# Squared-ReLU feed-forward after retention: the second product with its weights stationary and 192 tokens moving

## The chip, the cores and the metric

The kernel runs on one core of a Trainium2 chip. The metric is the device time of one execution in microseconds (us). The profiled execution is a single one, taken by the hardware profiler; its engines are called TensorE (PE; its weight loads PEld), VectorE (DVE), ScalarE (ACT), GpSimd (POOL) and SyncE (SP), whose queue issues nearly all DMAs here.

## The reference

```python
# q, k, v: (8, 8, 576, 64) float32; w_in: (512, 2048), w_out: (2048, 512)
scores = scale * np.matmul(q, k.transpose(0, 1, 3, 2))
Dmat = np.where(rel >= 0, gamma[:, None, None] ** rel[None, :, :], 0.0)
attn_out = np.matmul(scores * Dmat[None, :, :, :], v)
x = attn_out.transpose(0, 2, 1, 3).reshape(B * S, H * D)     # (4608, 512)
h = np.maximum(x @ w_in, 0.0)
return (h * h @ w_out).astype(np.float32)                    # (4608, 512)
```

All of it is float32. The weights come in as 64-bit floats, which the kernel reads as 64-bit integers and converts itself.

## The kernel before

The 4,608 tokens are nine blocks of 512. The work has two stages.

The first stage (up to about 548 us) computes retention in chunks of 128 tokens and, block by block, g = relu(x w_in)^2. It also loads w_out in sixteen pieces (`fetch_w`, L204, source pattern `piece_src`, L184), converts them on VectorE and forms seven combinations of its quarters, twice over: the result, `w2_dram`, holds for each of seven outer products the seven inner right operands. A piece is asked for when the piece three before it is finished (L275). g is written to DRAM as `g_dram`: of each half-block of 256 tokens' operand combinations five are kept (`G_KEPT`: A11, S1, A12, S3, A22). The order in this stage is written out by hand: `ffn` (L801) hands out a number of steps for each chunk, and a step carries the DMA issues that are due.

The second stage (L922 to L1128) computes g w_out by a scheme that replaces eight block products by seven (`PRODUCTS`, L27), on two levels. The outer level splits a block's tokens in two halves of 256, w_out's 2,048 rows in two and its 512 columns in two. The left operands are A11, S2, S1, A12, S3, S4, A22 of g. Five are read by `fetch_g` (L940) into one of six buffers `A(k)`; S2 and S4 are made on VectorE as differences of two others (`made`, L947, four quarters each). The inner level does the same again: `inner_sums` (L962) forms S1 to S4 of the quarters of A(k) on VectorE, and `inner(k, i)` (L1003) does inner product i. Each is four matmuls over chunks of 128 rows: 128 tokens of g stationary, 128 columns of w_out moving (L1017), so a result has tokens on the partitions. `k` counts outer products: nine blocks times seven, 63, and the blocks are taken in the order 1 to 8, then 0.

The inner results stay in three accumulators in PSUM per k and are combined with `p1`, `u2` and `p15`: product 0 and 3 leave through ScalarE (L1025, L1031), the others by an addition on VectorE (L1027 to L1037) into `r`. `outer` (L1068) adds `r` into the output tile on VectorE (L1079) and sends out a finished half-block of 256 tokens in one DMA on SyncE's queue (L1083). The very last product goes by `last_inner` (L1039), which adds quarter by quarter and sends each off.

The loop at L1104 sets the order. In iteration k TensorE gets inner products 0, then 4 of k - 1, 1 of k, 5 of k - 1, 2 of k, 6 of k - 1, 3 of k. Between them VectorE's queue gets the inner sums of k + 1, differences for k + 2, and steps of `sums_0` (L981), which forms S1 and S3 of block 0 from stored quarters (L996). At the end of an iteration the operand of k + 4 is asked for. The weights of the outer product j lie in `w_out[j]`, read by `fetch_w2` (L616).

At the border of the stages the last block's steps carry the first reads of g, the four inner sums of product 0 and four differences for product 1 (L1087 to L1099).

Of the kernel before, what the change touches and what calls it, by code (L numbers as in the profile page):

```python
# [17 lines left out]
TOK = 512  # L18
# [18 lines left out]
CLOSES = {3, 5, 6}  # L37


@with_exitstack  # L40
def kernel(
# [142 lines left out]
    def piece_src(j):  # L184
        wi, m, e = pieces[j]
        f = (m + e * N_M) * 128
        if wi == 0:
            return moe_w_in.rearrange("(c p) f -> p c f", p=128)[:, :, f:f + 128]
        return moe_w_out[f:f + 128, :].rearrange("p (c f) -> p c f", c=N_DM)
# [14 lines left out]
    def fetch_w(j):  # L204
        if j < len(pieces) and wide:
            nc.sync.dma_start(raw_of(j).bitcast(I64).rearrange("p (c f) -> p c f", c=N_DM), piece_src(j))
# [4 lines left out]
    def round_parts(j):  # L211
        words = raw_of(j).bitcast(U32).rearrange("p (n two) -> p n two", two=2)
        lo, hi = words[:, :, 0], words[:, :, 1]
        exp = exp_of(j).bitcast(U32)
        t = piece_dst(j)
        bits = t.bitcast(U32)

        def one():
            nc.vector.tensor_scalar(exp, hi, 20, 0x7FF, op0=ALU.logical_shift_right, op1=ALU.bitwise_and)

        def two():

            nc.vector.tensor_scalar(bits, as_dst(j, hi), 0xFFFFF, 0x100000, op0=ALU.bitwise_and, op1=ALU.bitwise_or)

        def beside():

            nc.scalar.activation(exp, exp, AF.Relu, bias=exp_bias[:, 0:1], scale=2.0 ** 23)

        def three():
            nc.vector.scalar_tensor_tensor(t, as_dst(j, lo), 2.0 ** -32, bits, op0=ALU.mult, op1=ALU.add)  # L230

        def four():
            nc.vector.scalar_tensor_tensor(t, t, 2.0 ** -20, as_dst(j, exp_of(j)), op0=ALU.mult, op1=ALU.mult)

        def five():
            nc.vector.scalar_tensor_tensor(bits, as_dst(j, hi), 0x80000000, bits, op0=ALU.bitwise_and, op1=ALU.bitwise_or)

        if not wide:
            to = t if pieces[j][0] == 0 else t.rearrange("p o s f -> p (o s) f")
            return [lambda: nc.sync.dma_start(to, piece_src(j))] + [lambda: None] * 5  # L240
        return [one, two, beside, three, four, five]
# [374 lines left out]
    def fetch_w2(j):  # L616
        nc.sync.dma_start(w_out[j].rearrange("p m s f -> p m (s f)"), w2_dram[WO_SLOT[PRODUCTS[j][1]], :, :, :])
# [310 lines left out]
    def part(at):  # L928
        return room[:, at:at + N_M * HT]

    A_room = [late.tile([128, N_M * HT], F32, name=f"a{j}") for j in range(4)] + [part(2048), part(4096)]
    s_room = [part(11776), part(0), part(13824)]
    o_room = [part(at).rearrange("p (h j d) -> p h j d", h=2, j=2) for at in (7168, 9216)]
    N_K = N_BLK * NP
    BLOCKS = list(range(1, N_BLK)) + [0]

    def A(k):
        return A_room[k % len(A_room)].rearrange("p (m t) -> p m t", m=N_M)

    def fetch_g(k):  # L940

        j = k % NP
        if k < N_K and j not in (2, 5):
            k += j == 1
            nc.sync.dma_start(A(k), g_dram[BLOCKS[k // NP], G_KEPT.index(PRODUCTS[k % NP][0]), :, :, :])

    def made(k):  # L947

        if k >= N_K or k % NP not in (1, 5):
            return []  # L950
        x, y = (k + 1, k - 1) if k % NP == 1 else (k - 2, k - 4)
        at = [slice(2 * e, 2 * e + 2) for e in range(4)]
        return [lambda at=at: nc.vector.tensor_tensor(A(k)[:, at, :], A(x)[:, at, :], A(y)[:, at, :], op=ALU.subtract) for at in at]

    def lefts(k):

        x = A(k)
        t = s_room[k % 3].rearrange("p (s m t) -> p s m t", s=4, m=N_MQ)
        return dict({f"S{e + 1}": t[:, e, :, :] for e in range(4)},
                    A11=x[:, 0:N_MQ, 0:128], A12=x[:, N_MQ:, 0:128], A21=x[:, 0:N_MQ, 128:], A22=x[:, N_MQ:, 128:])  # L960

    def inner_sums(k):  # L962

        if k >= N_K:
            return [None] * 4
        x = lefts(k)
        return [
            lambda: nc.vector.tensor_tensor(x["S1"], x["A21"], x["A22"], op=ALU.add),
            lambda: nc.vector.tensor_tensor(x["S2"], x["S1"], x["A11"], op=ALU.subtract),
            lambda: nc.vector.tensor_tensor(x["S3"], x["A11"], x["A21"], op=ALU.subtract),  # L970
            lambda: nc.vector.tensor_tensor(x["S4"], x["A12"], x["S2"], op=ALU.subtract),
        ]
# [3 lines left out]
    def bank(name):  # L976
        n_bank[0] += 1
        pool, tag = (ps_f, "f") if n_bank[0] % 8 < 3 else (ps_g, "g")
        return pool.tile([128, 512], F32, tag=tag, name=name)[:, 0:128]

    def sums_0():  # L981

        for m in range(N_M):
# [9 lines left out]
            for _ in range(6):  # L993
                yield None
# [3 lines left out]
            for _ in range(3):  # L998
                yield None

    state = {}

    def inner(k, i):  # L1003

        n, j = divmod(k, NP)
        o = o_room[n % 2]
        if i == 0:
            small = late3.tile([128, 3, 128], F32, tag="small", name="small")
            r = o[:, 0, :, 0:HT] if j == 0 else late2.tile([128, 2, HT], F32, tag="r", name="r")
            state[k] = dict(r=r, lefts=lefts(k), p1=small[:, 0, :], u2=small[:, 1, :], p15=small[:, 2, :])  # L1010
# [5 lines left out]
        for m in range(N_MQ):  # L1016
            nc.tensor.matmul(p, lhsT=s["lefts"][left][:, m, :], rhs=w_out[j][:, m, WO_SLOT[right], :],  # L1017
# [3 lines left out]
        if k == N_K - 1:  # L1021

# [7 lines left out]
        elif i == 3:  # L1030
            nc.scalar.copy(r[:, 0, 0:128], p)  # L1031
        elif i == 4:
            nc.vector.tensor_tensor(r[:, 1, 128:], p, s["p15"], op=ALU.add)
        elif i == 5:
            nc.vector.tensor_tensor(r[:, 0, 128:], p, s["u2"], op=ALU.add)
        else:
            nc.vector.tensor_tensor(r[:, 1, 0:128], p, s["p1"], op=ALU.add)  # L1037

    def last_inner(s, i, p):  # L1039
        n = N_BLK - 1  # L1040
        o = o_room[n % 2]
        c21 = o[:, 1, :, 0:HT]
        add = lambda to, x, y: nc.vector.tensor_tensor(to, x, y, op=ALU.add)
        at = {3: (0, 0), 4: (1, 1), 5: (0, 1), 6: (1, 0)}
        place = lambda e: c21[:, at[e][0], 128 * at[e][1]:128 * at[e][1] + 128]
        if i == 0:
            nc.scalar.copy(s["p1"], p)
        elif i == 1:
            add(s["u2"], p, s["p1"])
            add(s["u2"], s["u2"], place(5))  # L1050
        elif i == 2:
            add(s["p15"], p, s["p1"])
            add(s["p15"], s["p15"], place(4))
            add(s["p1"], s["p1"], place(6))
        else:
            add(place(i), p, {3: place(3), 4: s["p15"], 5: s["u2"], 6: s["p1"]}[i])
        def leave(rows, cols):
            row = BLOCKS[n] * TOK + HT + rows * 128
            nc.sync.dma_start(out[row:row + 128, cols], o[:, 1, rows, cols])

        if i == 3:
            leave(0, slice(HT, TOK))
            leave(1, slice(HT, TOK))
        if i >= 3:
            rows, c = at[i]
            leave(rows, slice(128 * c, 128 * c + 128))

    def outer(k):  # L1068

        if k == N_K - 1:  # L1070
            return
        n, j = divmod(k, NP)
        r = state.pop(k)["r"]
        o = o_room[n % 2]
        c11, c12 = o[:, 0, :, 0:HT], o[:, 0, :, HT:]
        c21, c22 = o[:, 1, :, 0:HT], o[:, 1, :, HT:]
        for to, with_ in {1: [(c21, c11)], 2: [(c12, c21)], 3: [(c11, c11)], 4: [(c22, c12), (c21, c21)],
                          5: [(c12, c12)], 6: [(c21, c21)]}.get(j, []):
            nc.vector.tensor_tensor(to, r, with_, op=ALU.add)  # L1079
        if j >= 5:  # L1080
            half = j - 5
            row = BLOCKS[n] * TOK + half * HT
            nc.sync.dma_start(out[row:row + HT, :].rearrange("(a p) d -> p a d", p=128), o[:, half, :, :])  # L1083
# [3 lines left out]
    while steps:  # L1087
        n, f, *args = steps[0]
        if n == N_BLK - 1:
            if n_last in (0, 5, 10, 15):  # L1090
                fetch_g(n_last // 5)
            if n_last in (2, 9, 16, 23):
                fetch_w2(2 + n_last // 7)
            if n_last == N_MP * NP - 5:
                for f in inner_sums(0):
                    f()
            if n_last >= N_MP * NP - 4:
                made(1)[n_last - N_MP * NP]()
# [5 lines left out]
    for k in range(N_K + 1):  # L1104
        sums_g = [None] * (k % NP == NP - 1) + made(k + 2)
        assert k + 4 < N_K - NP or next(steps_0, None) is None
        sums_next = inner_sums(k + 1)
        if k < N_K:
            inner(k, 0)
        for e in range(3):  # L1110
            if k > 0:
                inner(k - 1, 4 + e)
            if e == 2 and k > 0:
                outer(k - 1)
            if k < N_K:
                inner(k, 1 + e)
            if sums_next[e]:
                sums_next[e]()
            if sums_g:
                f = sums_g.pop(0)  # L1120
            else:
                f = next(steps_0, None)
            f and f()
        if sums_next[3]:
            sums_next[3]()
        for f in sums_g:
            f()
        fetch_g(k + 4)  # L1128
# [46 lines left out]
```

## Time and profile before

| | |
|---|---|
| time, median of 3 runs | 947.91 us (946.22 to 948.93) |
| profiled execution, its own time | 948.14 us |
| its span, first to last instruction | 946.4 us |
| mean granted TensorE clock | 0.998 |
| TensorE busy | 936.4 us (99%) |
| weight loads busy | 843.4 us (89%) |
| VectorE busy | 764.1 us (81%) |
| ScalarE busy | 353.9 us (37%) |
| GpSimd busy | 83.1 us (9%) |
| moved by DMA | 181.42 MB |

The profile's page lists groups of instructions by line of code, with count, busy time and mean duration of one. The views by time say what an engine did in a stretch. A busy matmul is not a matmul at its peak: its end is modelled and overlaps the next one, so what counts is the distance from one start to the next. The same holds in part for VectorE. The chain of work that ended last is followed back from the last instruction, at each step to what released it; 95% of it is TensorE.

### The profile page before, as it was taken

The numbers are of one execution on the slowest core, as the hardware profiler recorded it, in microseconds if no ns is written. First come the engines' busy times: TensorE is split into PE (matmuls) and PEld (weight loads), VectorE is DVE, ScalarE is ACT, GpSimd is POOL, SyncE is SP. The second block draws the span as 40 slices with busy tenths as digits, with TensorE's granted clock in tenths as the row PEclk, the third lists the DMA queues.
The fourth block names the chain that finished last, engine by engine and source line by source line (L and its number), as shares of the span: only waits on it lengthen the run. The fifth ranks groups of instructions, "written<-read, shape, count | busy, mean of one in ns | idle before, by whom it ended". The sixth has DMA issues, their size and how long they took to land.

```text
span 946.4 us, 23257 instructions
## 1 busy us (share of the span) xinstructions
PE 936.4 (99%) x9724; PEld 843.4 (89%) x9724; DVE 764.1 (81%) x1419; ACT 353.9 (37%) x831; POOL 83.1 (9%) x82
## 2 busy tenths in 40 slices
PE   8999999999999999999999999999999999999998
PEld 7554878888888888888888899999999999999998
DVE  5978699979797988888846688888878788787876
ACT  3557767676676686676621110000000000000000
POOL 3223011111111111220000000000000000000000
PEclk9999999999999999999999999999999999999999
DMA  9997475686468565863569983544555453525241
GB/s 223 230 281 194 143 196 144 193 289 190 148 201 273 176 190 163 276 190 117 186 224 361 347 294 124 189 161 142 192 179 185 158 206 107 201 101 178 110 160 46
DMA packets 173673, 181.42 MB, mean 192 GB/s; under 512 B 119168, under 2 KB 134400, under 8 KB 166912
## 3 DMA queue, kind: packets, MB, share of 16 engines
q1 hardware_dynamic: 171472, 179.41, 59.8%
q8 instruction: 76, 1.25, 0.5%
q10 hardware_dynamic: 2096, 0.52, 0.3%
q14 instruction: 29, 0.24, 0.1%
HBM read 109.39 MB, written 70.52 MB: 190 GB/s over the span
## 4 chain that ended last, share of the span: by engine, by line
PE 95%; DVE 3%; DMA 1%; ACT 0%; issue 0%; SPq 0%; DVEq 0%
PE o_b L1017 18%; PE h_b L706 17%; PE o_c L1017 12%; PE o_a L1017 12%; PE h_a L706 12%; PE h_c L706 11%; PE h_ps L668 6%; PE x_ps L565 3%; PE sc_ps L471 2%; PE x_ps L600 1%; PE u_ps L559 1%; DMA q_ld<-in_q_dram 1%; PE sc_ps L500 0%; PE t_ps L436 0%; PE x_ps L526 0%
## 5 line engine op out<-in xcount | busy, mean ns | idle before, releaser
L706 PE MATMUL h_b<-room,w 128*128 128x256 f32 x768 | 181.6, 379 | 1.3 <-DVE room L725 1.3
L422 ACT COPY qk<-flip 32x256 f32<-32x256 f32 x432 | 173.8, 402 | 6.7
L706 PEld LDWEIGHTS h_b<-room,w 128*128 128x128 f32 x768 | 145.7, 190 | 21.8 <-DVE room L725 2.1
L1017 PE MATMUL o_b<-w,room 128*128 128x128 f32 x1168 | 144.1, 275 | 0.0
L1017 PEld LDWEIGHTS o_b<-w,room 128*128 128x128 f32 x1168 | 137.2, 192 | 0.0
L706 PE MATMUL h_a<-room,w 128*128 128x256 f32 x512 | 124.4, 386 | 0.0
L1017 PE MATMUL o_c<-w,room 128*128 128x128 f32 x1008 | 123.0, 275 | 0.0
L706 PE MATMUL h_c<-room,w 128*128 128x256 f32 x512 | 121.0, 379 | 0.0
L1017 PEld LDWEIGHTS o_c<-w,room 128*128 128x128 f32 x1008 | 117.7, 192 | 0.0
L1031 ACT COPY r<-o_a 128x128 f32<-128x128 f32 x53 | 14.1, 266 | 271.4 <-PE o_a L1017 230.3
L706 PEld LDWEIGHTS h_c<-room,w 128*128 128x128 f32 x512 | 97.3, 190 | 13.2
L706 PEld LDWEIGHTS h_a<-room,w 128*128 128x128 f32 x512 | 95.3, 191 | 13.9
L1017 PE MATMUL o_a<-w,a 128*128 128x128 f32 x688 | 85.7, 275 | 0.0
L1017 PEld LDWEIGHTS o_a<-w,a 128*128 128x128 f32 x688 | 81.2, 192 | 0.1
L713 DVE SCALAR_TENSOR_TENSOR room<-room 128x512 f32<-128x512 f32 x96 | 68.4, 713 | 3.3
L387 POOL TENSOR_TENSOR q_ld<-q_ld,dv 128x512 f32<-128x512 f32 x34 | 39.3, 1155 | 292.0 <-DMA q_ld<-in_q_dram 259.1
L668 PE MATMUL h_ps<-room,w 128*128 128x512 f32 (+1 forms) x152 | 57.7, 532 | 0.2
L565 PEld LDWEIGHTS x_ps<-qk,v_ld 64*64 64x64 f32 x1024 | 39.4, 136 | 12.7 <-issue 11.2
L565 PE MATMUL x_ps<-qk,v_ld 64*64 64x64 f32 x1024 | 49.8, 223 | 0.0
L668 PEld LDWEIGHTS h_ps<-room,w 128*128 128x128 f32 x152 | 26.0, 190 | 26.5 <-issue 25.3
L486 POOL TENSOR_TENSOR v_ld<-v_ld,dv 128x512 f32<-128x512 f32 x36 | 42.1, 1169 | 76.4 <-DMA v_ld<-in_v_dram 66.0
L492 ACT COPY u_sb<-u_ps 128x256 f32<-128x256 f32 x60 | 22.5, 375 | 67.7 <-PE u_ps L559 62.5
(111 smaller groups left out, 1304.2 us busy)
## 6 DMA issues: line engine op xcount, KB each, us to landing
g_dram<-room SPq DMA_DIRECT2D x164, 256.0 KB, 3.8
a<-g_dram SPq DMA_DIRECT2D x30, 1024.0 KB, 5.9
room<-g_dram SPq DMA_DIRECT2D x15, 1024.0 KB, 6.2
w_dram<-w SPq DMA_DIRECT2D x28, 448.0 KB, 4.7
w<-w_dram SPq DMA_DIRECT2D x7, 1792.0 KB, 11.2
out_dram<-room SPq DMA_DIRECT2D x17, 512.0 KB, 3.3
q_ld<-in_q_dram SPq DMA_DIRECT2D x64, 128.0 KB, 3.8
w<-in_moe_w_in_dram SPq DMA_DIRECT2D x16, 512.0 KB, 6.1
```

Source lines behind the costliest of these rows:

```text
L387: engine.tensor_tensor(t, t, dv[:, heads, at:at + 1].to_broadcast(list(t.shape)), op=ALU.mult)
L422: nc.scalar.copy(*moves.pop(0)[2:])
L471: nc.tensor.matmul(st[i]["sc"][e][rows(h), hp, :], lhsT=st[i]["kT"][rows(e), hp, t], rhs=st[i]["qT"][rows(e), hp, t], start=True, stop=Tru ...
L486: nc.gpsimd.tensor_tensor(vs, vs, dv[:, :, at:at + 1].to_broadcast([C, H, D]), op=ALU.mult)
L492: nc.scalar.copy(u_sb[(2 * i + h + 1) % 3], u_ps[0])
L559: return [lambda hp=hp, e=e, b=b: nc.tensor.matmul(u[rows(e), hp, :], lhsT=loaded[i][1][rows(h), 2 * hp + e, :], rhs=st[i]["vs"][rows(h), ...
L565: return [lambda hp=hp, e=e, b=b: nc.tensor.matmul(x_at(hp, e, b, h), lhsT=s["vs"][rows(h), head(hp, e), :], rhs=s["ret"][rows(h), e, hp, ...
L668: nc.tensor.matmul(p, lhsT=w[:, c, :], rhs=xT[0][:, c, :].rearrange("p (h t) -> p h t", h=2)[:, lo:hi, at[0]:at[1]], start=(c == 0), stop= ...
L706: nc.tensor.matmul(p[:, mm, :], lhsT=w[:, c, :], rhs=xs[n][right][:, c, :], start=(j in OPENS and mm == 0 and c == 0), stop=(j in CLOSES a ...
L713: nc.vector.scalar_tensor_tensor(t, t, 0.0, t, op0=ALU.max, op1=ALU.mult)
L1017: nc.tensor.matmul(p, lhsT=s["lefts"][left][:, m, :], rhs=w_out[j][:, m, WO_SLOT[right], :], start=(i in OPENS and m == 0), stop=(i in CLO ...
L1031: nc.scalar.copy(r[:, 0, 0:128], p)
```

## The change

The second product is turned. Now w_out's 128 columns are stationary and the tokens of g move, 192 at a time, so a result has w_out's columns on the partitions and tokens along the free dimension. The nine blocks' two token halves are cut anew into six groups, each of 384 tokens of one half and 384 of the other (768 tokens); a group can span two blocks, so reads of g and writes of the output are cut at block borders (`runs`). There are 42 outer products in place of 63.

The outer products are taken in another order (`OUTER`: S1, A11, S2, A12, S4, S3, A22), with four buffers A(k) of 1.5 MB in place of six of 1 MB, read in a LOW and a HIGH half. Two inner-sum slots per product in place of four: S3 and S4 overwrite S1 and S2, and are formed in product k itself. The output quarters X, Y, Z are combined in that order. A finished quarter is turned on VectorE by squares of 32 (`nc.vector.transpose`, into one of three `t_room` tiles) one iteration later and leaves by four DMAs per run of tokens, one for each 32 partitions. For these squares to give whole pieces of rows, the columns of w_out are laid out anew when it is loaded: a piece of w_out comes by four DMAs in place of one. At the end, the DMAs alternate between SyncE's and ScalarE's queues.

```diff
+OUTER = [PRODUCTS[j] for j in (2, 0, 1, 3, 5, 4, 6)]
...
-        return moe_w_out[f:f + 128, :].rearrange("p (c f) -> p c f", c=N_DM)
+        return moe_w_out[f:f + 128, :].rearrange("p (o b s c) -> o s p b c", o=2, b=4, s=2)
...
+            to = to.rearrange("p (o s b c) -> o s p b c", o=2, s=2, b=4)
+            for o in range(2):
+                for s in range(2):
+                    nc.sync.dma_start(to[o, s], piece_src(j)[o, s])
...
+    TC = 3 * HT // 2
+    NQ = TC // 2
+    N_K = N_BLK * HT // TC * NP
...
+    def fetch_g(k, ms):
+        if k < N_K and OUTER[k % NP][0] in G_KEPT:
+            for b, t, c, w in runs(k // NP):
+                nc.sync.dma_start(A(k)[:, ms, c:c + w], g_dram[b, G_KEPT.index(OUTER[k % NP][0]), :, ms, t:t + w])
...
+        x, y = (k - 2, k - 1) if k % NP == 2 else (k - 1, k - 2)
+        at = [(LOW, RIGHT), (HIGH, RIGHT), (LOW, LEFT), (HIGH, LEFT)]
...
+    def leave(k, o, h, e, es, lo, hi, both=False):
+        t = t_room[n_left[0] % 3]
+        n_left[0] += 1
+        for i in range(es.start, es.stop):
+            nc.vector.transpose(t[:, 0:(hi - lo) // 32, i, :], o[:, i, lo:hi])
+        for b, at, c, w in runs(k // NP, lo, hi):
+            row = b * TOK + h * HT + at
+            to = out[row:row + w, e * HT:(e + 1) * HT].rearrange("(a r) (p e c) -> p r a e c", r=32, e=2, c=32)[:, :, :, es, :]
+            lo_ = (c - lo) // 32
+            for p in range(4):
+                own = slice(32 * p, 32 * p + 32)
+                queue_ = nc.scalar if both and p % 2 else nc.sync
+                queue_.dma_start(to[p], t[own, lo_:lo_ + w // 32, es, :])
...
-            nc.tensor.matmul(p, lhsT=s["lefts"][left][:, m, :], rhs=w_out[j][:, m, WO_SLOT[right], :],
+            nc.tensor.matmul(p, lhsT=w_out[j][:, m, WO_SLOT[right], :], rhs=s["lefts"][left][:, m, :],
...
+        for to, x, with_ in {2: [(Z, r, X), (Y, Y, Z)], 3: [(X, r, X)], 4: [(X, r, Y)], 5: [(Y, r, Y), (Z, r, Z)],
+                             6: [(Z, r, Z)]}.get(j, []):
+            nc.vector.tensor_tensor(to, x, with_, op=ALU.add)
+        if j >= 3:
+            o, h, e = {3: (X, 0, 0), 4: (X, 0, 1), 5: (Y, 1, 1), 6: (Z, 1, 0)}[j]
+            leaving.append(lambda: leave(k, o, h, e, slice(0, 2), 0, TC, k == N_K - 2))
...
             if n_last == N_MP * NP - 5:
-                for f in inner_sums(0):
-                    f()
-            if n_last >= N_MP * NP - 4:
-                made(1)[n_last - N_MP * NP]()
+                inner_sum(0, "S1")
+                inner_sum(0, "S2")
...
+        extras = {0: [0, 1], 1: [2, None, 3], 2: [0, 1, 2], 3: [None, 3]}.get(j, [])
...
         if k < N_K:
             inner(k, 0)
         for e in range(3):
             if k > 0:
                 inner(k - 1, 4 + e)
-            if e == 2 and k > 0:
-                outer(k - 1)
+            if e == 2:
+                inner_sum(k + 1, "S2")
+                if 0 < k < N_K:
+                    outer(k - 1)
             if k < N_K:
                 inner(k, 1 + e)
+            if e == 1:
+                inner_sum(k, "S3")
+                inner_sum(k, "S4")
+            extra(e)
+            if e == 0:
+                inner_sum(k + 1, "S1")
+                while leaving:
+                    leaving.pop(0)()
+        fetch_g(k + 3, HIGH)
+        fetch_g(k + 4, LOW)
```

More of the change, by code (lines that the diff above doesn't have):

```diff
@@ L205, in fetch_w @@
         if j < len(pieces) and wide:
-            nc.sync.dma_start(raw_of(j).bitcast(I64).rearrange("p (c f) -> p c f", c=N_DM), piece_src(j))
+            to = raw_of(j).bitcast(I64)
+            if pieces[j][0] == 0:
+                nc.sync.dma_start(to.rearrange("p (c f) -> p c f", c=N_DM), piece_src(j))
+                return
+            to = to.rearrange("p (o s b c) -> o s p b c", o=2, s=2, b=4)
+            for o in range(2):
+                for s in range(2):
+                    nc.sync.dma_start(to[o, s], piece_src(j)[o, s])
     def round_parts(j):
@@ L238, in round_parts @@
         if not wide:
-            to = t if pieces[j][0] == 0 else t.rearrange("p o s f -> p (o s) f")
-            return [lambda: nc.sync.dma_start(to, piece_src(j))] + [lambda: None] * 5
+            if pieces[j][0] == 0:
+                moves_ = [(t, piece_src(j))]
+            else:
+                moves_ = [(t[:, o, s, :].rearrange("p (b c) -> p b c", b=4), piece_src(j)[o, s]) for o in range(2) for s in range(2)]
+            return [lambda: [nc.sync.dma_start(*m) for m in moves_]] + [lambda: None] * 5
         return [one, two, beside, three, four, five]
@@ L616, in fetch_w2 @@
     def fetch_w2(j):
-        nc.sync.dma_start(w_out[j].rearrange("p m s f -> p m (s f)"), w2_dram[WO_SLOT[PRODUCTS[j][1]], :, :, :])
+        nc.sync.dma_start(w_out[j].rearrange("p m s f -> p m (s f)"), w2_dram[WO_SLOT[OUTER[j][1]], :, :, :])
     sums_x = {}
@@ L926 @@
     ps_g = ctx.enter_context(tc.tile_pool(name="ps_g", bufs=5, space=PS))
[L928 to L934, printed above, removed]
-    BLOCKS = list(range(1, N_BLK)) + [0]
-    def A(k):
-        return A_room[k % len(A_room)].rearrange("p (m t) -> p m t", m=N_M)
@@ L940, in fetch_g @@
[L940 to L945, printed above, removed]
-    def made(k):
[L949 to L953, printed above, removed]
+    TC = 3 * HT // 2
@@ new lines @@
+    NQ = TC // 2
+    N_K = N_BLK * HT // TC * NP
+    assert N_K * TC == N_BLK * HT * NP
+    BLOCKS = list(range(1, N_BLK)) + [0]
+    size = N_M * TC
+    A_room = [late.tile([128, size], F32, name=f"a{j}") for j in range(2)] + [room[:, at:at + size] for at in (5888, 11776)]
+    s_room = [late.tile([128, N_M * NQ], F32, name="s0"), room[:, 10240:10240 + N_M * NQ]]
+    X, Y, Z = (room[:, at:at + 2 * TC].rearrange("p (e t) -> p e t", e=2) for at in (0, 2 * TC, 4 * TC))
+    t_room = [room[:, at:at + 2 * TC].rearrange("p (a e c) -> p a e c", e=2, c=32) for at in (2304, 3072, 3840)]
@@ new lines, with runs @@
+    LOW, HIGH = slice(0, N_MQ), slice(N_MQ, N_M)
+    LEFT, RIGHT = slice(0, NQ), slice(NQ, TC)
+    def A(k):
+        return A_room[k % 4].rearrange("p (m t) -> p m t", m=N_M)
+    def runs(n, lo=0, hi=TC):
+        while lo < hi:
+            b, t = divmod(n * TC + lo, HT)
+            w = min(HT - t, hi - lo)
+            yield BLOCKS[b], t, lo, w
+            lo += w
+    def fetch_g(k, ms):
+        if k < N_K and OUTER[k % NP][0] in G_KEPT:
+            for b, t, c, w in runs(k // NP):
+                nc.sync.dma_start(A(k)[:, ms, c:c + w], g_dram[b, G_KEPT.index(OUTER[k % NP][0]), :, ms, t:t + w])
@@ L955, in lefts @@
+    def made(k):
+        if k >= N_K:
+            return [None] * 4
+        x, y = (k - 2, k - 1) if k % NP == 2 else (k - 1, k - 2)
+        at = [(LOW, RIGHT), (HIGH, RIGHT), (LOW, LEFT), (HIGH, LEFT)]
+        return [lambda m=m, t=t: nc.vector.tensor_tensor(A(k)[:, m, t], A(x)[:, m, t], A(y)[:, m, t], op=ALU.subtract)
+                for m, t in at]
     def lefts(k):
         x = A(k)
-        t = s_room[k % 3].rearrange("p (s m t) -> p s m t", s=4, m=N_MQ)
-        return dict({f"S{e + 1}": t[:, e, :, :] for e in range(4)},
-                    A11=x[:, 0:N_MQ, 0:128], A12=x[:, N_MQ:, 0:128], A21=x[:, 0:N_MQ, 128:], A22=x[:, N_MQ:, 128:])
@@ L962, in inner_sums @@
[L962 to L972, printed above, removed]
+        t = s_room[k % 2].rearrange("p (s m t) -> p s m t", s=2, m=N_MQ)
@@ new lines, in lefts, with inner_sum @@
+        return dict({f"S{e + 1}": t[:, e % 2, :, :] for e in range(4)},
+                    A11=x[:, LOW, LEFT], A12=x[:, HIGH, LEFT], A21=x[:, LOW, RIGHT], A22=x[:, HIGH, RIGHT])
+    INNER = {"S1": ("A21", "A22", ALU.add), "S2": ("S1", "A11", ALU.subtract),
+             "S3": ("A11", "A21", ALU.subtract), "S4": ("A12", "S2", ALU.subtract)}
+    def inner_sum(k, name):
+        if 0 <= k < N_K:
+            x = lefts(k)
+            a, b, op = INNER[name]
+            nc.vector.tensor_tensor(x[name], x[a], x[b], op=op)
@@ L978, in bank @@
         pool, tag = (ps_f, "f") if n_bank[0] % 8 < 3 else (ps_g, "g")
-        return pool.tile([128, 512], F32, tag=tag, name=name)[:, 0:128]
+        return pool.tile([128, 512], F32, tag=tag, name=name)[:, 0:NQ]
     def sums_0():
@@ L992, in sums_0 @@
             yield lambda: move(QUARTERS, False)
-            for _ in range(6):
+            for _ in range(4):
                 yield None
@@ L997, in sums_0 @@
             yield lambda: move(SUMS, True)
-            for _ in range(3):
+            for _ in range(2):
                 yield None
     state = {}
+    leaving = []
+    n_left = [0]
+    def leave(k, o, h, e, es, lo, hi, both=False):
[11 more added lines that the diff above has]
+                queue_.dma_start(to[p], t[own, lo_:lo_ + w // 32, es, :])
     def inner(k, i):
         n, j = divmod(k, NP)
-        o = o_room[n % 2]
         if i == 0:
-            small = late3.tile([128, 3, 128], F32, tag="small", name="small")
-            r = o[:, 0, :, 0:HT] if j == 0 else late2.tile([128, 2, HT], F32, tag="r", name="r")
+            small = late3.tile([128, 3, NQ], F32, tag="small", name="small")
+            r = (Y, X)[j] if j < 2 else late2.tile([128, 2, TC], F32, tag="r", name="r")
             state[k] = dict(r=r, lefts=lefts(k), p1=small[:, 0, :], u2=small[:, 1, :], p15=small[:, 2, :])
@@ L1020, in inner @@
         r = s["r"]
-        if k == N_K - 1:
+        if k == N_K - 1 and i >= 3:
             last_inner(s, i, p)
@@ L1030, in inner @@
         elif i == 3:
-            nc.scalar.copy(r[:, 0, 0:128], p)
+            nc.scalar.copy(r[:, 0, LEFT], p)
         elif i == 4:
-            nc.vector.tensor_tensor(r[:, 1, 128:], p, s["p15"], op=ALU.add)
+            nc.vector.tensor_tensor(r[:, 1, RIGHT], p, s["p15"], op=ALU.add)
         elif i == 5:
-            nc.vector.tensor_tensor(r[:, 0, 128:], p, s["u2"], op=ALU.add)
+            nc.vector.tensor_tensor(r[:, 1, LEFT], p, s["u2"], op=ALU.add)
         else:
-            nc.vector.tensor_tensor(r[:, 1, 0:128], p, s["p1"], op=ALU.add)
+            nc.vector.tensor_tensor(r[:, 0, RIGHT], p, s["p1"], op=ALU.add)
@@ L1039, in last_inner @@
     def last_inner(s, i, p):
-        n = N_BLK - 1
-        o = o_room[n % 2]
-        c21 = o[:, 1, :, 0:HT]
         add = lambda to, x, y: nc.vector.tensor_tensor(to, x, y, op=ALU.add)
[L1044 to L1056, printed above, removed]
@@ L1057, in leave @@
-        def leave(rows, cols):
-            row = BLOCKS[n] * TOK + HT + rows * 128
-            nc.sync.dma_start(out[row:row + 128, cols], o[:, 1, rows, cols])
-        if i == 3:
[L1062 to L1066, printed above, removed]
+        at = {3: (0, LEFT), 4: (1, RIGHT), 5: (1, LEFT), 6: (0, RIGHT)}
+        place = lambda i: Z[:, at[i][0], at[i][1]]
+        own = {4: s["p15"], 5: s["u2"], 6: s["p1"]}
@@ L1068, in outer @@
+        if i == 3:
+            for e in (4, 5, 6):
+                add(own[e], own[e], place(e))
+        add(place(i), p, own.get(i, place(3)))
+        e, t = at[i]
+        if i != 3:
+            leave(N_K - 1, Z, 1, 0, slice(0 if i == 5 else e, e + 1), t.start, t.stop, True)
     def outer(k):
-        if k == N_K - 1:
-            return
         n, j = divmod(k, NP)
         r = state.pop(k)["r"]
-        o = o_room[n % 2]
-        c11, c12 = o[:, 0, :, 0:HT], o[:, 0, :, HT:]
-        c21, c22 = o[:, 1, :, 0:HT], o[:, 1, :, HT:]
@@ L1077, in outer @@
[L1077 to L1083, printed above, removed]
+        for to, x, with_ in {2: [(Z, r, X), (Y, Y, Z)], 3: [(X, r, X)], 4: [(X, r, Y)], 5: [(Y, r, Y), (Z, r, Z)],
+                             6: [(Z, r, Z)]}.get(j, []):
+            nc.vector.tensor_tensor(to, x, with_, op=ALU.add)
@@ L1089 @@
         if n == N_BLK - 1:
-            if n_last in (0, 5, 10, 15):
-                fetch_g(n_last // 5)
+            if n_last in (0, 5):
+                fetch_g(n_last // 5, slice(0, N_M))
+            if n_last == 10:
+                fetch_g(3, LOW)
             if n_last in (2, 9, 16, 23):
@@ L1104, with extra @@
     for k in range(N_K + 1):
-        sums_g = [None] * (k % NP == NP - 1) + made(k + 2)
+        j = k % NP
+        if j in (0, 2):
+            parts = made(k + 2)
+        extras = {0: [0, 1], 1: [2, None, 3], 2: [0, 1, 2], 3: [None, 3]}.get(j, [])
         assert k + 4 < N_K - NP or next(steps_0, None) is None
-        sums_next = inner_sums(k + 1)
+        def extra(e):
+            own = [parts[extras[e]]] if e < len(extras) and extras[e] is not None else []
+            for f in own + [next(steps_0, None)]:
+                f and f()
         if k < N_K:
@@ L1112 @@
                 inner(k - 1, 4 + e)
-            if e == 2 and k > 0:
-                outer(k - 1)
+            if e == 2:
+                inner_sum(k + 1, "S2")
+                if 0 < k < N_K:
+                    outer(k - 1)
             if k < N_K:
                 inner(k, 1 + e)
[L1117 to L1128, printed above, removed]
+            if e == 1:
[8 more added lines that the diff above has]
+        fetch_g(k + 4, LOW)
 def _decays(B, H, S, D):
```

## The prediction

> **What bounds the kernel now.** I read first the busy time by stretch, cut where the second product begins (548.6 us) and where its last matmul ends (columns: length; busy of TensorE, its weight loads, VectorE, ScalarE, GpSimd; clock; DMA share; GB/s).
>
> ```profile
> 446.00:548.60 102.60, 102.60 (x767) 90.04 (x766) 70.25 (x110) 30.75 (x65) 1.06 (x1) 1.00 0.77 277
> 548.60:942.73 394.13, 394.12 (x3529) 393.93 (x3527) 320.22 (x718) 33.27 (x125) 0.00 (x0) 1.00 0.45 159
> 942.73:946.40 3.67, 0.00 (x0) 0.00 (x0) 0.29 (x1) 0.00 (x0) 0.00 (x0) 0.98 0.43 131
> ```
>
> The second product is 394.13 us of matmuls without a gap at full clock, then 3.67 us of tail. "x3529" is 63 outer x 7 inner x 4 chunks = 1,764 matmuls, each recorded as two float32 passes: 3,528. So 394.13 / 3,528 = 111.7 ns from start to start. The chain of work that ended last gives the same around the border of the stages (start, length, what):
>
> ```profile
> 531.50 1.73 PE h_b L706 x8
> 533.23 1.73 PE h_c L706 x8
> ...
> 551.44 1.79 PE o_a L1017 x16
> 553.23 1.79 PE o_b L1017 x16
> ```
>
> Moving 128 columns: 1.79 / 16 = 111.8 ns. Moving 256 (L706): twelve such runs, 526.32 to 547.04, are 20.72 us, 215.8 ns each. Twice the columns cost 1.93 times. Moving 512 (L668), from the weight loads in the timeline:
>
> ```profile
> 60.38 0.19 PEld L668 LDWEIGHTS h_ps<-room,w 128*128 128x128 f32 x1 [0.24 <-issue]
> ...
> 64.24 0.19 PEld L668 LDWEIGHTS h_ps<-room,w 128*128 128x128 f32 x1 [0.24 <-issue]
> ```
>
> Nine loads in 3.86 us: 428.9 ns. From 256 to 512 a column costs (428.9 - 215.8) / 256 = 0.832 ns and about 2.7 ns stay over; at 128 that line gives 109.3, the trace 111.7. Only the narrow shape pays something extra.
>
> VectorE is second (320.22 of 394.13). Its busy time counts overlapping tails; what a job occupies is start to start:
>
> ```profile
> 704.21 0.69 DVE L971 TENSOR_TENSOR room<-a,room 128x512 f32<-128x512 f32 x1
> 704.81 0.68 DVE L953 TENSOR_TENSOR a<-a,room 128x512 f32<-128x512 f32 x1
> 705.41 0.28 DVE L1033 TENSOR_TENSOR r<-o_b,small 128x128 f32<-128x128 f32 x1
> 705.61 0.28 DVE L1027 TENSOR_TENSOR small<-o_b,small 128x128 f32<-128x128 f32 x1
> 705.81 0.68 DVE L968 TENSOR_TENSOR room<-a 128x512 f32<-128x512 f32 x1
> ...
> 302.77 0.70 DVE L407 STREAM_TRANSPOSE flip<-k_ld 128x512 f32<-128x512 f32 x1
> 303.40 0.65 DVE L646 TENSOR_TENSOR room<-room 128x512 f32<-128x512 f32 x1
> ```
>
> 512 columns occupy 0.605 us, 128 columns 0.20, a square-wise transpose of 512 columns 0.63: 1.055 ns a column plus 0.065 (0.09 for the transpose).
>
> **The change part by part.**
>
> *Matmuls.* 6 groups x 7 x 7 x 4 x 2 = 2,352 instructions of 192 columns replace 3,528 of 128; the columns are the same 451,584. The trace has no 192. The line through 256 and 512 gives 215.8 - 64 x 0.832 = 162.5 ns; halfway between the measured 128 and 256 it would be 163.7. I take 162.5, because the extra of the 128 shape looks like the weight load (weight loads are back to back there, with gaps at 512), and one load per 162 ns has room. 2,352 x 162.5 = 382.2: **-11.9 us** (-9.1 at 163.7).[...]
>
> *VectorE.* A product is 7 x 4 x 2 = 56 passes, 56 x 162.5 = 9.10 us, so a group of seven leaves VectorE 63.7 us. Its jobs, with 768 columns at 0.875 us, 192 at 0.268, 384 transposed at 0.495: 28 inner sums 24.5; 35 additions from PSUM 9.4; 8 quarters of differences 7.0; 7 outer additions 6.1; 8 new transposes 4.0. Sum 51.0 of 63.7 (80%); now 28 x 0.605 + 35 x 0.20 + 8 x 0.605 + 7 x 0.605 = 33.0 of 43.8 (75%). On average it fits. The order is what can fail: S2 of the next product is queued behind seven waiting steps of this one. Index 0 of a group is worst (two differences, two transposes, an outer addition). With PE steps of 1.30 us from the product's start: u2 4.1 to 4.4 (its matmuls end at 3.9, results 0.2 later), difference 5.2, S1 6.1, transposes 7.1, additions 7.7, S3 8.5, S4 9.4, difference 10.3, addition 10.5, S2 11.4. PE wants it at 9.10 + 2.60 = 11.7. S3 at 8.5 is wanted at 10.4. So 0.3 us are to spare, less 0.35 where a sum for block 0 (L996, 0.42) falls in.[...] By the rows 0 to 1; I take **+0.5**.
>
> *First product.* S1 and S2 alone are made ahead; from 551.3 us on VectorE has 0.54 of additions and six jobs of 0.875 before S2 of the second product, 557.1; PE wants it after six steps, 548.6 + 7.8 = 556.4; with 0.1 for the hand-over **+0.8** (0 to 1.5).
>
> *Reads of g and the queue.* Bytes stay: 30 x 1.5 MB for 45 x 1 MB. Four buffers for six, filled in halves; the second half is asked for one product and 4 us before its sums, 13 us ahead, landing about 6 (median of L945). Both ends: 0, or a stall if the queue is late. SyncE's queue now holds, after each leave (waiting for its transposes, the reads of g queued behind), 8 output DMAs and 4 reads. Issue times (ns, min/median/max):
>
> ```profile
> L1083 SPq DMA_DIRECT2D out_dram<-room x17: 378/389/389, 590.6 to 940.3; - x17
> L945 SPq DMA_DIRECT2D a<-g_dram x30: 319/351/626, 502.7 to 907.9; - x30
> L157 SPq DMA_DIRECT2D q_ld<-in_q_dram x80: 384/607/3075, 1.2 to 431.9; - x80
> ```
>
> 8 x 0.45 + 4 x 0.35 = 5.0 of 9.1 us, in four products of seven. Issue starts near 7.1, so the reads leave at 12.2, 3 us into the next product, and land at 9; their sums come 5 us later. The output leaves in pieces of 256 bytes, 36,864 of them, as the loads of q, k and v do (the page's 119,168 packets under 512 B). The first 100 us, full of those, moved 220 GB/s at a DMA share of 0.91; at that rate 159 GB/s would take a share of 0.66. **0**.
>
> *ScalarE* still copies twice a product, 192 wide, and sits at 33 of 394: 0.
>
> *First stage.* Each of 16 pieces of w_out comes by four DMAs instead of one: 48 more issues on SyncE, about 0.5 us each, one piece in some 19 us, ahead of stores of g and loads of q, k, v. Pieces are asked for three ahead and TensorE shows no gap there: 0, at worst 1.5 in all.
>
> *Tail.* Now 3.67 us: the last addition, then issues, then landing:
>
> ```profile
> 942.16 2.21 SPq L1059 DMA_DIRECT2D out_dram<-room  x4
> 942.76 0.29 DVE L1043 TENSOR_TENSOR room<-o_b,small 128x128 f32<-128x128 f32 x1 [0.60 <-PE o_b L1017]
> ```
>
> After, each last quarter is transposed (0.3) and leaves by 4 or 8 small DMAs on two queues, with Y before: 24 issues, 12 a queue at about 0.5 = 6, from 1.3 us before the last matmul's end, 4.7 after it, and 2 for landing: 6.7. Without queueing: addition and transpose 0.7, two issues 1.0, landing 2, hand-overs 1.0: 4.7. I take 5.9: **+2.2** (+1.0 to +3.5).
>
> Sum: -11.9 + 0.5 + 0.8 + 2.2 = -8.4. The profiled execution took 948.14 (span 946.4), so 939.7; it lies 0.2 above the median, 947.91, so **939.5**.
>
> **The rivals.**
> *VectorE's order binds.* S2 is late at index 0 and the lateness runs on into index 1[...]. For: only 0.3 us of slack. Against: back-to-back jobs occupy 0.605, not 0.69.
>
> *The queue binds, slower.* Place: SyncE's queue in the four leaving products. Four products of 12 issues outrun 9.1 us each only above 0.76 us an issue; the reads have about 5 us to spare, so at c a group stalls 4 x (12c - 9.1) - 5, five groups have reads behind. It eats the gain of 8.4 at c = 0.90 and at 1.0 costs 33: **972**. For: q loads took up to 3.1[...]. Against: medians 0.35 to 0.61.
>
> *The change doesn't do what it says.* If the extra of the 128 shape is per column, 192 costs 1.5 x 111.7 = 167.5, nothing is won, and the costs remain: **951.4**. Against it stands the 256 row.
>
> **How the numbers follow.** Main case 0.72, from 936 (no cost but the cadence) to 943 (163.7 ns and the larger tail); VectorE 0.15, 941 to 946; queue 0.06; no cadence 0.04; the rest, 0.03, near no change. The range, 936 to 945, takes in the first and most of the second. A measurement tells 0.3%, 2.8 us: faster 0.87, within 0.05, slower 0.08.
>
> **What would show it.** In the profile after: chain pieces of 8 matmuls at 1.30 us, TensorE's second stage at 382 to 384 with 2,352 instructions; no wait of TensorE on VectorE beyond 1 us but at the start; VectorE near 80% there; output issues under 0.6 us; a tail of 5 to 7 us. Wrong it is if the 8 take over 1.33, if S2 at index 0 recurs as what TensorE waits for, or if TensorE waits for reads of g.

## The result and the profile after

| | before | after |
|---|---|---|
| median | 947.07 us (6 runs) | 942.12 us (6 runs) |
| ratio after to before | | 0.9944, 95% interval 0.9920 to 0.9968 |
| profiled execution, its own time | 948.14 us | 941.51 us |
| span | 946.4 us | 939.8 us |
| second product, first matmul to last end | 394.12 us | 384.32 us |
| from there to the end | 3.70 us | 8.17 us |

Faster by 0.56%, 5.0 us (the interval reaches from 3.0 to 7.6); predicted were 8.4 us less and 939.5, with 936 to 945 as the range. The time is inside the range, the gain is about 60% of the one forecast. The end of the first stage moves from run to run: it lay between 547.3 and 551.9 us in the ten profiles of this case. The two latest, of the runs ends and turn2 below, had a granted clock of 0.98 from 100 to 200 us; before, after, t128 and b_wload had 1.00. So the profiles are compared from the first matmul of the second product on: 397.8 us before, 392.5 after, 5.3 less, which agrees with the medians.

The busy time by stretch, cut at the first and the last matmul of the second product (columns as in the prediction):

```profile
547.29:931.61 384.32, 382.89 (x2353) 382.01 (x2351) 318.10 (x536) 26.46 (x83) 0.00 (x0) 1.00 0.57 160
931.61:939.80 8.19, 0.00 (x1) 0.00 (x0) 1.23 (x5) 0.00 (x0) 0.00 (x0) 0.75 0.47 90
```

The matmuls shrank by 9.8 us and the tail grew by 4.5. The chain of work, in the middle of the stage (start, length, what):

```profile
600.57 2.60 PE o_b L1053 x16
603.17 2.60 PE o_c L1053 x16
605.77 1.30 PE o_b L1053 x8
```

A pass takes 1.30 / 8 = 162.5 ns, as the line through 256 and 512 columns said. 2,352 of them are 382.2 us; the 2.1 us beyond that are waits and the last result's way out. TensorE waits twice, near the start and before the last inner product (timeline; in brackets the wait and who ended it):

```profile
555.09 0.95 DVE L992 TENSOR_TENSOR room<-room,a 128x768 f32<-128x768 f32 x1
...
556.10 1.57 PE L1053 MATMUL o_b<-room,w 128*128 128x192 f32 x8 [0.85 <-DVE room L992]
...
930.04 1.57 PE L1053 MATMUL o_b<-a,w 128*128 128x192 f32 x8 [0.58 <-DVE room L1075]
```

The first is S2 of the second product, done about 0.95 us after 555.09. From start to start the two cost 1.01 and 0.74 us beyond the 162.5, and about 0.1 more each in the restart. Between them, over 373 us, TensorE never waits. VectorE in index 0 of a group, that is in the first of its seven outer products:

```profile
681.27 0.95 DVE L975 TENSOR_TENSOR a<-room 128x768 f32<-128x768 f32 x1
682.14 0.35 DVE L1072 TENSOR_TENSOR r<-o_b,small 128x192 f32<-128x192 f32 x1
682.40 0.95 DVE L992 TENSOR_TENSOR room<-room 128x768 f32<-128x768 f32 x1
683.27 0.95 DVE L1093 TENSOR_TENSOR room<-r,room 128x768 f32<-128x768 f32 x1
```

The third row is S2 of the next outer product. It ends at 683.35, and the matmuls that read it start at 683.60, on time. Start to start a job of 768 columns occupies 0.87 us.

The tail: after the last addition the transposes, and the two queues' issues (how many, over how long):

```profile
930.43 7.39 SPq L1038 DMA_DIRECT2D out_dram<-room  x12
...
930.43 6.01 ACTq L1038 DMA_DIRECT2D out_dram<-room  x12
...
932.49 0.38 DVE L1030 STREAM_TRANSPOSE room<-room 128x192 f32<-128x192 f32 x1
```

SyncE's last issue ends 6.2 us after the last matmul; landing and the end of the program take 2.0 more. The twelve issues on SyncE do not fill the 7.39 us. From 930 us on, their durations (ns, min/median/max) and what the queue stood for (us in total, times, longest):

```profile
L1038 SPq DMA_DIRECT2D out_dram<-room x12: 315/394/468, 930.4 to 937.4; - x12
SPq L1038 <- DMA out_dram<-room: 2.2, 4, 0.8
```

Twelve times 394 ns are about 4.7 us. For 2.2 us the queue stood until an earlier output DMA had landed.

### The profile page after: what moved, and what is told of

Its sections match the earlier page's. It is cut to its first block, busy times and chain, and to the rows that moved or that the text cites. A ratio compares the mean times of both kernels' runs of the same rounds, so it can differ in the third digit from the quotient of the medians.

```text
span 939.8 us, 21110 instructions
## 1 busy us (share of the span) xinstructions
PE 925.0 (98%) x8548; PEld 830.6 (88%) x8548; DVE 759.9 (81%) x1235; ACT 346.9 (37%) x789; POOL 83.3 (9%) x82
## 4 chain that ended last, share of the span: by engine, by line
PE 93%; DVE 4%; DMA 1%; ACT 1%; issue 0%; DVEq 0%; SPq 0%
PE h_b L717 17%; PE o_b L1053 17%; PE h_a L717 12%; PE o_c L1053 11%; PE h_c L717 11%; PE o_a L1053 11%; PE h_ps L679 6%; PE x_ps L576 3%; PE sc_ps L482 2%; PE x_ps L611 1%; PE u_ps L570 1%; DMA k_ld<-in_k_dram 1%; DVE w L244 0%; PE t_ps L447 0%; DVE room L992 0%
## 5 line engine op out<-in xcount | busy, mean ns | idle before, releaser
L1053 PE MATMUL o_b<-room,w 128*128 128x192 f32 x496 | 90.8, 326 | 0.8 <-DVE room L992 0.8
L1053 PEld LDWEIGHTS o_b<-room,w 128*128 128x128 f32 x496 | 82.3, 190 | 1.1 <-DVE room L992 1.1
L1053 PE MATMUL o_a<-a,w 128*128 128x192 f32 x352 | 62.6, 326 | 0.0
L1053 PE MATMUL o_b<-s,w 128*128 128x192 f32 x336 | 61.5, 326 | 0.0
L1053 PE MATMUL o_c<-s,w 128*128 128x192 f32 x336 | 61.5, 326 | 0.0
L1053 PE MATMUL o_c<-room,w 128*128 128x192 f32 x336 | 61.5, 326 | 0.0
L1053 PEld LDWEIGHTS o_a<-a,w 128*128 128x128 f32 x352 | 58.1, 190 | 0.1
L1053 PE MATMUL o_a<-room,w 128*128 128x192 f32 x320 | 56.9, 326 | 0.0
L1053 PEld LDWEIGHTS o_c<-s,w 128*128 128x128 f32 x336 | 55.8, 190 | 0.0
L1053 PEld LDWEIGHTS o_c<-room,w 128*128 128x128 f32 x336 | 55.8, 190 | 0.0
```

Source lines behind the costliest of these rows:

```text
L1053: nc.tensor.matmul(p, lhsT=w_out[j][:, m, WO_SLOT[right], :], rhs=s["lefts"][left][:, m, :], start=(i in OPENS and m == 0), stop=(i in CLO ...
```

## The experiments

Eight kernels were run. Ratios are to the kernel before in the same session, whose median was 947.05 us for t128, b_wload, turn2 and ends, and 947.42 for w96, turn2_first, ends2 and ends3.

**t128: the turn without the width.**

```diff
-    TC = 3 * HT // 2
+    TC = HT
```

> The changed kernel with groups of 512 tokens (TC = HT): turned as in the change, but 128 tokens moving and 63 outer products. Theory (the gain is the cadence of the wider shape and nothing else): 3,528 matmuls at 111.7 ns = 394 us again, no gain, and the costs of the change stay (start about 1, tail 2 to 4): 1.003 to 1.006 of before, about 950 to 953 us. Rival (the turn itself gains, w_out as the stationary operand loads or streams better): well below 111.7 ns per matmul, 940 to 944 us.

Measured: 954.46 us, ratio 1.0070 (1.0057 to 1.0083), a little above the range given. The chain, between waits:

```profile
701.20 1.79 PE o_c L1053 x16
702.99 0.89 PE o_b L1053 x8
703.88 1.79 PE o_a L1053 x16
```

Again 1.79 / 16 = 111.9 ns, with w_out stationary as with g stationary. The matmuls' stretch is 398.9 us (394.12 before), the tail 6.3 (3.70): 7.4 in all, as the medians say. The 4.8 us in the stretch are waits for VectorE: 0.8 each at two places at the start and one at the end, 0.1 to 0.2 once or twice a group, and 0.1 after each for the restart. So everything in the change but the width costs 7.4 us at the old width, and the width brings all the gain: 954.46 down to 942.12.

**w96: narrower still.**

```diff
-    TC = 3 * HT // 2
+    TC = 3 * HT // 4
```

> The changed kernel with groups of 384 tokens, so 96 tokens moving, 84 outer products and 4,704 passes over the same columns. Theory (below some width the pass is bound by its weight load, which costs the same whatever moves: that is the extra of the 128 shape): 107 to 112 ns a pass where nothing waits, 505 to 527 us of matmuls, about 1,065 to 1,085 us in all. Rival (the extra of the 128 shape is a matter of columns, 0.83 to 0.87 ns each): 82 to 84 ns a pass where nothing waits, about 390 us plus waits for VectorE, 945 to 970 us.

Measured: 1081.37 us (2 runs), ratio 1.1405 (1.1372 to 1.1439), as the theory had it. The chain, and the busy time over 510 us of the stage:

```profile
701.51 1.79 PE o_a L1053 x16
703.29 1.79 PE o_b L1053 x16
705.08 1.79 PE o_c L1053 x16
```

```profile
560.00:1070.00 510.00, 510.00 (x4570) 510.00 (x4569) 353.65 (x1015) 38.76 (x162) 0.00 (x0) 1.00 0.44 119
```

96 columns take the same 111.9 ns as 128, without a wait. So a pass has a floor here, the same for 96 and 128 columns. That the weight load makes it is not shown: the loads are busy all the time in both shapes (510.00 of 510.00 us here, 393.93 of 394.13 at 128 in the kernel before), but nearly so at 192 too (382.01 of 384.32), and no run here changed the load itself. The line 0.832 N + 2.7 ns meets 111.8 at 131 columns (an estimate from the 256 and 512 shapes): 128 columns lie just under that corner, so a third fewer loads was worth 3% of this stage and not a third.

**b_wload: the first stage's part alone, in the kernel before.**

```diff
-        return moe_w_out[f:f + 128, :].rearrange("p (c f) -> p c f", c=N_DM)
+        return moe_w_out[f:f + 128, :].rearrange("p (o b s c) -> o s p b c", o=2, b=4, s=2)
...
+            to = to.rearrange("p (o s b c) -> o s p b c", o=2, s=2, b=4)
+            for o in range(2):
+                for s in range(2):
+                    nc.sync.dma_start(to[o, s], piece_src(j)[o, s])
```

> The kernel before with w_out loaded as in the change, four DMAs of 256-byte pieces per piece in place of one; the output's columns are left in the changed order. Theory (the first stage hides it): the time of before within 1 us, the first stage ending at 547 to 549 us. Rival (the first stage pays for the 48 issues and the small pieces, and this is why the median gained less than the profile): 1 to 3 us slower than before, the first stage ending later and TensorE waiting there.

Measured: 946.94 us, ratio 0.9999 (0.9991 to 1.0006), the stage ending at 548.3. The 48 more issues cost at most 0.6 us, the upper end of the interval.

**turn2: every transpose twice.**

```diff
-            nc.vector.transpose(t[:, 0:(hi - lo) // 32, i, :], o[:, i, lo:hi])
+            for _ in range(2):
+                nc.vector.transpose(t[:, 0:(hi - lo) // 32, i, :], o[:, i, lo:hi])
```

> The changed kernel with every transpose on VectorE done twice: about 0.97 us more per leaving product, all else equal. Theory (S2 at index 0 of a group has only about 0.3 us to spare): TensorE waits for S2 at index 0 of groups 1 to 5 for 0.6 to 0.9 us each, 3 to 4.5 us, and about 1 us more at the tail: 4 to 5.5 us above the changed kernel, about 946 to 948 us. Rival (VectorE at about 80% has room in general): only the tail, about 1 us above the changed kernel.

Measured: 951.63 us, ratio 1.0056 (1.0039 to 1.0073): 9.5 above the changed kernel, about twice what was expected. The rival fell. The waits are where they were expected and also next to them. The second stretch is 392.87 us, 8.5 longer; the matmuls for S2 start 1.03 us late (and 0.1 for the restart) at index 0 of groups 1 to 5, and 0.2 to 0.8 late at index 1. What TensorE's matmuls waited for (us in total, times, longest; the second row holds the first product's wait too, which the changed kernel also has):

```profile
PE o_b L1054 <- DVE s L992: 3.3, 4, 0.9
PE o_b L1054 <- DVE room L992: 3.3, 5, 0.9
```

And VectorE at index 0 (the third row holds four transposes):

```profile
749.15 0.95 DVE L992 TENSOR_TENSOR s<-room 128x768 f32<-128x768 f32 x1
750.02 2.26 DVE L1031 STREAM_TRANSPOSE room<-room 128x384 f32<-128x384 f32 x4
...
755.57 0.95 DVE L992 TENSOR_TENSOR s<-s,room 128x768 f32<-128x768 f32 x1
```

Four occupy 2.18 us to the next job (752.20), where two took 0.96: 1.22 more, not 0.97. S2's matmuls are 1.03 late and restart 0.1 slower, so what was to spare was 0.1 to 0.2 us.

**turn2_first: turn2's work, S2 earlier in the queue.**

```diff
             if e == 2:
-                inner_sum(k + 1, "S2")
+                if j:
+                    inner_sum(k + 1, "S2")
...
                 inner_sum(k, "S3")
+                if j == 0:
+                    inner_sum(k + 1, "S2")
                 inner_sum(k, "S4")
```

> The kernel with every transpose twice, and S2 of the next product put ahead of S4 and of the second difference in VectorE's queue at index 0 of each group. Same work on every engine. Theory (the 8.5 us of waits come from the place of S2 in the queue, not from VectorE's load): S2 is ready 1.7 us earlier at index 0, the five waits of 1.1 us go, those at index 1 shrink, 5 to 8 us below the kernel with doubled transposes, 944 to 947 us. Rival (VectorE is short of time at index 0 and 1 whatever the order): 950 to 952 us as before the reordering.

Measured: 948.77 us, ratio 1.0013 (1.0005 to 1.0021), between theory and rival. The five waits at index 0 go, those at index 1 grow from 2.7 to 5.7 us with their restarts. In one group:

```profile
758.04 0.94 DVE L992 TENSOR_TENSOR s<-room 128x768 f32<-128x768 f32 x1
...
759.03 1.57 PE L1054 MATMUL o_b<-s,w 128*128 128x192 f32 x8 [0.54 <-DVE s L992]
...
760.03 0.95 DVE L992 TENSOR_TENSOR room<-room 128x768 f32<-128x768 f32 x1
...
761.03 1.57 PE L1054 MATMUL o_b<-room,w 128*128 128x192 f32 x8 [0.44 <-DVE room L992]
```

These are S3 and S2 formed in index 1. They are late because index 0 now holds more work than its 9.1 us: by start-to-start times seven jobs of 0.87, four transposes in 2.18 and five additions of about 0.26 make 9.6 us (an estimate from the rows above), and the rest is handed on. The stretch is 389.3 us, 3.6 less than turn2's. But 1.1 of these are the wait in the first product, which the changed kernel has too and which this order removes with the others. So of the 8.5 us that doubling the transposes added, about 2.5 were order and 6 load. The claim that order alone decides does not stand.

**ends: both ends reordered, same work.**

```diff
+        if k == 0:
+            extras = [None, 0, 1]
...
+            if final:
+                last_outer(4 + e)
+            if final and e < 2:
+                inner_sum(k, f"S{3 + e}")
...
-                if 0 < k < N_K:
+                if 0 < k < N_K - 1:
                     outer(k - 1)
...
                 inner_sum(k, "S3")
+                if k == 0:
+                    inner_sum(1, "S2")
                 inner_sum(k, "S4")
```

(`last_outer` adds to Y and Z quarter by quarter; S3 and S4 of the last product use the free slot.)

> The changed kernel with both ends reordered: at k = 0 S1 and S2 of product 1 go ahead of the differences; at the last product S3 and S4 are formed early in the free slots, and the last outer additions to Y and Z are done quarter by quarter as the quarters come, so that Y leaves before the last quarters are added. Theory (the start costs 1.1 us, the wait before the last inner product 0.9, and the tail is bound by 12 issues a queue that begin too late): the first wait gone, the last gone, the tail about 5 in place of 7.7: 3.5 to 4.5 us below the changed kernel, about 938 us, ratio to before 0.990. Rival (the tail is landing and end of program, not issue): only the 2 us of waits are won, about 940 us.

Measured: 939.28 us, ratio 0.9922 (0.9907 to 0.9938), 2.8 below the changed kernel, between theory and rival. The wait at the start is gone, that at the end is 0.27, the stretch 382.7 us. The tail is 7.0, not 5. VectorE's last transpose waits:

```profile
934.69 0.36 DVE L1080 TENSOR_TENSOR room<-o_b,small 128x192 f32<-128x192 f32 x1 [0.47 <-PE o_b L1058]
937.07 0.38 DVE L1029 STREAM_TRANSPOSE room<-room 128x192 f32<-128x192 f32 x1 [2.02 <-DMA out_dram<-room]
```

With three tiles for transposes, the last transpose waited 2.02 us until an output DMA had landed.

**ends2: a fourth tile, X on both queues, the last quarter of Z later.**

```diff
-... for at in (2304, 3072, 3840)]
+... for at in (2304, 3072, 3840, 4608)]
...
-            leaving.append(lambda: leave(k, o, h, e, slice(0, 2), 0, TC, k == N_K - 2))
+            leaving.append(lambda: leave(k, o, h, e, slice(0, 2), 0, TC, k >= N_K - 3))
```

> The version with both ends reordered, and besides: X's last leave also on both queues, a fourth tile for transposes (so that the last transpose needs not wait 2 us for a DMA), the last quarter of Z added after the second to last inner results. Theory (the tail of 7 us is 12 issues a queue of 0.45 us behind X's eight issues on one queue): 1.2 to 2 us below that version, about 937.5 us. Rival (landing and end of program set the tail): no change, 939 us.

Measured: 938.32 us, ratio 0.9900 (0.9882 to 0.9919). That is 1.0 below ends, a little short of the theory's 1.2 to 2. The stretch is 382.36 us, 2,352 passes and the last result's way out. The tail is 6.75, only 0.3 less:

```profile
929.62:936.37 6.75, 0.00 (x0) 0.00 (x0) 0.74 (x2) 0.00 (x0) 0.00 (x0) 0.76 0.46 83
```

The transposes are now done 0.8 us after the last matmul, so the wait of the last transpose was not what held the tail. Twelve issues a queue still take 6.8 and 7.1 us from 927.23.

**ends3: three queues.**

```diff
-                queue_ = nc.scalar if both and p % 2 else nc.sync
+                queue_ = (nc.sync, nc.scalar, nc.gpsimd)[n_issue[0] % 3] if both else nc.sync
+                n_issue[0] += 1
```

> The same with the last leaves' DMAs spread over three queues, SyncE, ScalarE and GpSimd. Theory (issue-bound tail): eight issues a queue instead of twelve, 1 to 1.8 us below the two-queue version, about 936 us. Rival (GpSimd's issue is slow[...]): 0 to 5 us above the two-queue version.

Measured: 937.83 us, ratio 0.9895 (0.9876 to 0.9914); the medians differ by 0.5 and the intervals overlap, so the times alone don't tell the two apart. In the traces the stretch is 382.36 us in both, and the tail is 5.87 in place of 6.75:

```profile
929.65:935.52 5.87, 0.00 (x1) 0.00 (x0) 0.74 (x2) 0.00 (x0) 2.63 (x5) 0.90 0.49 96
```

That is the theory's direction, short of its 1 to 1.8; the rival's loss did not come. An issue took longer on GpSimd (ns, min/median/max):

```profile
L1045 SPq DMA_DIRECT2D out_dram<-room x179: 315/438/1890, 595.6 to 932.5; - x179
...
L1045 ACTq DMA_DIRECT2D out_dram<-room x11: 322/444/511, 922.8 to 931.2; - x11
L1045 POOL DMA_DIRECT2D out_dram<-room x10: 542/568/716, 923.1 to 931.7; - x10
```

This is the fastest version here, 4.3 us below the changed kernel's median, which was taken in another session.

## Why the prediction was right, and what was mis-sized

| step | predicted | measured in the trace |
|---|---|---|
| matmuls, 162.5 ns each | -11.9 | -11.9 |
| first product | +0.8 | +1.1 |
| S2 at index 0 | +0.5 | 0 |
| wait before the last inner product | not in the sum | +0.85 |
| reads of g, queue, first stage, ScalarE | 0 | 0 |
| tail | +2.2 | +4.5 |
| sum | -8.4 | -5.4 (-5.3 in the trace, -5.0 in the medians) |

*Matmuls.* Right to the tenth: t128 and w96 show that the gain is leaving a floor of 111.8 ns a pass, not the turn. That the weight load makes this floor was the author's estimate and is not shown. The loads were busy all the time before (393.93 of 394.13 us), a third of them went, and yet only 3% was to be had, since the line for moving columns lay only 2.4 ns under the floor at 128. At 96 columns that line gives 82.6 ns and the pass took 111.9, so there fewer passes do pay: from w96 to t128, a quarter fewer, the time fell by 127 us. So the busy share of the loads alone did not tell here what fewer loads bring.

*VectorE.* The hand-worked queue was right in its order and to about 0.1 us in its times: S2 was worked out 0.3 us before its need and ended 0.25 before its matmuls, about 0.1 before the weight load in front of them. By start to start 768 columns take 0.87 us (0.875 taken), where the duration shown is 0.95. Had a job occupied its whole duration, the six of 768 columns up to the end of S2 would have taken about 0.5 us more (an estimate, 6 x 0.08), and waits like those of turn2 would have come. The rival that VectorE's order binds, whose 941 to 946 us was the author's estimate, thus failed by only 0.1 to 0.2 us, and turn2 shows how steep the other side is: 1.22 us more per leaving product made the kernel 9.5 us slower. VectorE was busy 318 of 384 us, 83%.

*The queue.* Issues had a median of 438 ns on SyncE, eight in 3.8 to 4.9 us in the timeline, and TensorE never waited for a read of g. DMA share 0.57 (at most 0.66 was worked out). So the rival in which the queue binds did not come.

*The first product* was sized within 0.3 us; ends removed its wait by order alone.

*The wait before the last inner product* was missed. The last inner product adds onto the accumulator that VectorE must first read for inner product 4, and that read stands behind two outer additions of 768 columns and four of 192. The kernel before had jobs of 512 and 128 columns there, and no wait. It was luck that this miss and the +0.5 for a wait that did not come partly cancel.

*The tail* is the term that was mis-sized, and most of the 3 us by which the forecast was off. The prediction had two ends, 4.7 and 6.7 us, and took 5.9; measured were 8.2, above both, so its sign "a tail of 5 to 7 us" did not come. Twelve issues a queue were right, so was their start (1.2 us before the last matmul's end, 1.3 taken), and an issue was shorter than the 0.5 taken. What the sum put at nothing is time in which the queue stands between issues: they took 7.4 us on SyncE in place of 6, about 4.7 of issuing and 2.7 of standing, 2.2 of it until earlier output DMAs had landed. The last transpose ended at 932.87 and the last issue at 937.82, so in the last 5 us no transpose held the queue. Then came 2.0 for landing and the end of the program. The versions of the ends agree with this: reordering and a fourth tile brought 8.2 to 6.75, a third queue to 5.87, and t128, with eight issues a queue, had 6.3, so the number of issues on a queue is a part of it. Why an issue waits for an earlier landing no run here shows, and no run kept the kernel and changed only the number of output DMAs, so how the rest above the 3.7 us of before divides stays open.

## What to carry to other kernels

Measure the pass time at several widths of the moving operand before turning a product: for the float32 passes here 96 and 128 columns took the same 111.9 ns a pass, and from 128 to 192, past a corner at about 131 columns (an estimate from the line), a column became only 3% cheaper (162.5 ns for 192 in place of 111.7 for 128). The turned output cost time at the end of the program, where transposes, small DMAs and their issues stand uncovered (8.17 us after the last matmul in place of 3.70): list what is issued after the last matmul, divide it by queues, and add the time in which a queue stands until earlier transfers have landed (2.2 us on SyncE's queue here). And a VectorE queue at 80% can be one job away from the critical path (83% here, with 0.1 to 0.2 us to spare at index 0), so work the queue out job by job from start-to-start times.

## What was not expected of the hardware

A pass of 96 columns took 111.9 ns (w96), the same as 128 (t128). A square-wise transpose of 384 columns, repeated onto the same place, occupied 0.545 us (2.18 for four in turn2), where two onto different places took 0.96, 0.48 each, in the changed kernel; why was not tried. An issue of a DMA took 568 ns on GpSimd's queue against 438 on SyncE's and 444 on ScalarE's, of the same kind of transfer (ends3). At the end of the changed kernel, an issue on SyncE's queue stood up to 0.8 us until an earlier output DMA had landed.
